# Query transposes and output stores first in a chunk, loads held until a chunk begins, scores three half heads to a gap, in a fused attention and feed-forward kernel

## Chip, cores and metric

One core of a Trainium2 chip. The metric is the device time of one execution in us. Times of one kernel are compared with times of the kernel before taken in the same rounds on the same chip. Besides that, the granted TensorE clock of each run (1.0 is full speed) is used.

## The reference, cut to what matters

```python
# q, k, v: (8 batches, 8 heads, 576, 64); 4608 tokens of width 512; hidden width 1536
k_p = k.reshape(B, H, 72, 8, D).mean(axis=3)        # keys and values pooled by 8
v_p = v.reshape(B, H, 72, 8, D).mean(axis=3)
attn = softmax(q @ k_p^T / sqrt(D))                 # 576 x 72 per head
x = (attn @ v_p), heads side by side                # 4608 x 512
out = (relu(x @ w_gate) * (x @ w_val)) @ w_out      # 4608 x 512
```

## The kernel before

The feed-forward part runs in nine chunks of 512 tokens. While PE (TensorE) works through the units of chunk c, the attention of batch c + 1 is slipped into the gaps between units, and GpSimd (POOL) pools the keys and values of batch c + 2. A unit is one group of feed-forward matmuls, either for a block of the hidden layer or for a part of the output. From batch 2 on queries are transposed by DMA from SyncE's queue, and from batch 3 on so is each finished piece of attention on its way to `x_T`; before that TensorE transposes most of them. Names in the profile lines: qT are transposed queries, kp and kpT pooled keys, expT exponentials of the scores, px a finished piece of attention, h the hidden layer.

```python
ps_mm = tile_pool(bufs=4, PSUM); ps_at = tile_pool(bufs=3, PSUM)   # ps_at: scores and values

def scores(b, h):                       # one head = two halves, one PSUM tile each
    e = exp_pool.tile([P, 2, HS], F16, name="expT")
    for j, parts in enumerate(...):
        ps = ps_at.tile([P, 512], F32, ...)
        ...matmuls...
        nc.scalar.activation(out=e[:SP, j, :], in_=ps[:SP, :HS], func=AF.Exp, ...)

def values(b, t):                       # one piece of 128 (or 64) tokens: two PSUM tiles
    for half in range(2):
        ps = ps_at.tile([P, 512], F32, ...)
        ...four matmuls...
        nc.vector.reciprocal(...); nc.vector.tensor_tensor(out=x[...], in0=pv, in1=rd, op=mult)

def attention(b):                       # what goes into which gap
    ...
    if b == 2:
        pairs = [Sc[h:h + 2] for h in range(0, H, 2)]       # two heads to a gap
        ...
        return [[], [kt], []] + pairs + [v[:1], v[1:2], x[:1] + v[2:], x[1:2], x[2:], V[3:4], V[4:]]
    return [[kt], []] + [[p] for p in Sc + V]
...
for c in range(1, n_chunks):
    ...
    if c + 2 < B: prep(c + 2, c + 3 < B)                    # POOL: pooling, loads
    if c + 1 < B: others = attention(c + 1)
    if c + 2 < B: others[-1].append(lambda: q_dma(c + 2))   # query transpose, last gap
    for i, unit in enumerate(units):
        unit()
        ...run(sums[2 * i - 2:2 * i])                       # VectorE: eight sums of h
        if i < len(others): run(others[i])
```

The softmax here doesn't subtract the row's maximum and nothing guards it: scores larger than these inputs give would overflow.

## Time and profile before

| | before |
|---|---|
| device time, first three runs | 339.09, 339.21, 341.12 us |
| the profiled run | 341.79 us, span 340.0 us, clock 0.995 |
| PE busy | 96% of the span |
| work of a chunk with attention that waits for nothing | 33.80 us |
| excess of chunks 2, 3, 4 over it | 4.52, 0.76, 0.50 us |

The prediction shows the lines that the argument rests on. Part 2 of the page gives the wider view; each digit is the busy share, or the granted clock, of one of 40 slices of the span:

```profile
PE   7899999999969999999999999999999999999994
...
POOL 8446509999999900992199830000000000000000
PEclk9999999999979999999999999999999999999999
```

Between the start and the tail PE's row and the clock row have one dip each, both in slice 12; they are the hole in chunk 2 and what follows it. POOL runs as far ahead as its buffers let it and is finished by slice 24.

### The profile page before, as it was taken

To read this page: it belongs to the slowest core of one execution; us is meant where nothing else is said; L and a number is where in the kernel's file an instruction comes from. 1 tells how busy PE (TensorE), PEld (TensorE's weight loads), DVE (VectorE), ACT (ScalarE), POOL (GpSimd) and SP (SyncE) were. 2 spreads that over 40 slices of the span, in tenths; PEclk is the share of its full clock that TensorE was granted. 3 is DMA by queue.
4 is the path that set the end of the run, shared out by engine and by line. 5 is a ranking of instruction groups with operands and counts; after the bars stand their busy time and mean duration, and the time that the engine had idled before them with its cause. 6 is when DMAs were issued, how large, how long until landed. Compare 5 with 4: busy or idle time off the path is not lost.

```text
span 340.0 us, 6437 instructions
## 1 busy us (share of the span) xinstructions
PE 326.3 (96%) x2502; PEld 211.1 (62%) x2502; DVE 212.8 (63%) x450; ACT 128.4 (38%) x276; POOL 137.2 (40%) x182
## 2 busy tenths in 40 slices
PE   7899999999969999999999999999999999999994
PEld 2588875544536665666898866665666565555542
DVE  7465636759757676867675775677567554486520
ACT  1544562464236324632463246324632322232221
POOL 8446509999999900992199830000000000000000
PEclk9999999999979999999999999999999999999999
DMA  7999999946968099837990380037003600400143
GB/s 109 191 203 201 195 212 171 184 96 124 139 117 163 10 143 132 147 60 125 168 164 12 79 155 24 17 75 173 4 9 57 129 1 0 124 3 2 36 114 97
DMA packets 50550, 35.41 MB, mean 104 GB/s; under 512 B 30360, under 2 KB 44184, under 8 KB 50520
## 3 DMA queue, kind: packets, MB, share of 16 engines
q0 software_dynamic: 18304, 18.88, 34.8%
q1 hardware_dynamic: 32072, 16.00, 23.5%
q8 instruction: 19, 0.31, 0.4%
q10 hardware_dynamic: 144, 0.13, 0.1%
q14 instruction: 11, 0.09, 0.1%
HBM read 37.75 MB, written 9.44 MB: 139 GB/s over the span
## 4 chain that ended last, share of the span: by engine, by line
PE 87%; DMA 6%; DVE 2%; ACT 1%; issue 1%; POOL 1%; DVEq 0%; ACTq 0%; POOLq 0%
PE mm_ps L415 51%; PE acc_ps L515 18%; PE mm_ps L462 5%; DMA qT<-q 5%; PE at_ps L304 4%; PE at_ps L374 3%; DMA q<-in_q_dram 2%; DVE px L380 1%; PE mm_ps L564 1%; PE mm_ps L397 1%; PE mm_ps L278 1%; ACT expT L308 1%; DVE h L433 1%; PE mm_ps L327 1%; PE mm_ps L351 1%
## 5 line engine op out<-in xcount | busy, mean ns | idle before, releaser
L433 DVE TENSOR_TENSOR h<-mm_ps,relu 128x512 f16<-128x512 f32 (+2 forms) x120 | 76.7, 640 | 80.3 <-PE mm_ps L415 77.3
L421 ACT ACTIVATE relu<-mm_ps 128x512 f16<-128x512 f32 (+1 forms) x120 | 66.5, 554 | 129.6 <-PE mm_ps L415 128.9
L415 PE MATMUL mm_ps<-x_T,wv_sb 128*128 128x512 f16 (+1 forms) x528 | 113.7, 342 | 0.5 <-DVE h L433 0.5
L415 PE MATMUL mm_ps<-x_T,wg_sb 128*128 128x512 f16 (+1 forms) x528 | 114.0, 342 | 0.0
L415 PEld LDWEIGHTS <-wv_sb 128*128 128x128 f16 x528 | 51.7, 98 | 43.3 <-issue 1.9
L415 PEld LDWEIGHTS <-wg_sb 128*128 128x128 f16 x528 | 49.8, 98 | 28.2 <-issue 0.8
L308 ACT ACTIVATE expT<-at_ps 72x288 f16<-72x288 f32 x112 | 38.9, 403 | 26.3 <-PE at_ps L304 26.3
L515 PEld LDWEIGHTS <-sum 128*128 128x128 f16 x336 | 32.6, 98 | 6.2
L380 DVE TENSOR_TENSOR px<-at_ps,prd 128x256 f16<-128x256 f32 (+1 forms) x80 | 33.8, 423 | 2.7
L178 POOL TENSOR_TENSOR tree_b<-tree_a 72x256 f32<-72x256 f32 (+1 forms) x42 | 32.1, 763 | 3.3
L515 PE MATMUL acc_ps<-wo_sums,sum 128*128 128x256 f16 x252 | 30.9, 273 | 0.0
L172 POOL TENSOR_TENSOR tree_a<-v_in 72x512 f32<-72x512 f16 x24 | 29.2, 1217 | 0.1
L515 PEld LDWEIGHTS <-h 128*128 128x128 f16 x252 | 24.0, 98 | 4.0
L172 POOL TENSOR_TENSOR tree_a<-k_in 96x512 f32<-96x512 f16 x18 | 21.0, 1168 | 12.1 <-DMA k_in<-in_k_dram 12.1
L515 PE MATMUL acc_ps<-wo_sb,h 128*128 128x256 f16 x168 | 20.6, 273 | 0.0
L462 PE MATMUL mm_ps<-wo_sb,h 128*128 128x512 f16 x84 | 19.6, 379 | 0.0
L506 DVE TENSOR_TENSOR sum<-h 128x768 f16<-128x768 f16 x28 | 17.7, 674 | 0.2
L164 POOL DMA_DIRECT2D q<-in_q_dram x9 | 5.1, 561 | 30.4 <-issue 16.3
L523 DVE TENSOR_TENSOR rows<-acc_ps,mid 128x512 f32<-128x512 f32 x21 | 14.4, 688 | 4.5 <-PE acc_ps L515 3.8
L374 PEld LDWEIGHTS <-expT 72*128 72x128 f16 (+1 forms) x280 | 13.0, 100 | 6.2 <-ACT relu L421 1.1
L379 DVE RECIPROCAL prd<-at_ps 128x4 f32<-128x4 f32 (+1 forms) x80 | 13.7, 171 | 3.7 <-PE at_ps L374 3.6
L374 PE MATMUL at_ps<-stat,expT 72*128 72x65 f16 (+1 forms) x280 | 14.8, 194 | 0.0
(92 smaller groups left out, 286.3 us busy)
## 6 DMA issues: line engine op xcount, KB each, us to landing
out_dram<-rows SPq DMA_DIRECT2D x24, 256.0 KB
k_in<-in_k_dram POOLq DMA_DIRECT2D x7, 576.0 KB, 6.5
q<-in_q_dram POOLq DMA_DIRECT2D x7, 576.0 KB, 9.4
v_in<-in_v_dram POOLq DMA_DIRECT2D x6, 576.0 KB, 13.0
out_dram<-fout SPq DMA_DIRECT2D x7, 256.0 KB
wg_sb<-in_moe_w_gate_dram POOLq DMA_DIRECT2D x6, 256.0 KB, 12.1
wv_sb<-in_moe_w_val_dram POOLq DMA_DIRECT2D x6, 256.0 KB, 12.1
wo_sb<-in_moe_w_out_dram POOLq DMA_DIRECT2D x3, 512.0 KB, 10.1
```

Source lines behind the costliest of these rows:

```text
L172: eng.tensor_tensor(out=cell["a"][:n], in0=src[:, :, :4 * D], in1=src[:, :, 4 * D:], op=ALU.add)
L178: eng.tensor_tensor(out=cell["c"][:n], in0=a[:n, :, :2 * D], in1=a[:n, :, 2 * D:], op=ALU.add)
L308: nc.scalar.activation(out=e[:SP, j, :], in_=ps[:SP, :HS], func=AF.Exp, scale=EXP_SCALE)
L374: nc.tensor.matmul(out=ps[:n, c0:c0 + D + 1], lhsT=weights(b, h, t), rhs=stats[b % 2][:SP, g, s0:s0 + D + 1], start=True, stop=True,)
L380: nc.vector.tensor_tensor(out=x[:n, half * NG // 2:(half + 1) * NG // 2, :, :], in0=pv.rearrange("p g (x c) -> p g x c", x=2)[:, :, :, :D] ...
L415: nc.tensor.matmul(out=t[:, lo:hi], lhsT=w[:, ci, fsl], rhs=x_T[:, ci, x0:x0 + hi - lo], start=(ci == 0), stop=(ci == n_co - 1),)
L421: nc.scalar.activation(out=relu[:, :n], in_=ps[0][:, :n], func=AF.Relu)
L433: nc.vector.tensor_tensor(out=h, in0=val, in1=relu, op=ALU.mult)
L462: nc.tensor.matmul(out=t, lhsT=h_tiles[c][:, fo, ts * P:(ts + 1) * P], rhs=wo_sb[:, fo, :], start=(fo == 0), stop=(fo == n_fo - 1),)
L506: nc.vector.tensor_tensor(out=S[k][:, i], in0=x[:, i], in1=y[:, i], op=op)
L515: nc.tensor.matmul(out=ps[:, tb, :], lhsT=lhs[:, i, tb * P:(tb + 1) * P], rhs=rhs[:, i, :], start=(first and tb == 0 and i == 0), stop=(tb ...
L523: nc.vector.tensor_tensor(out=out_ap, in0=x, in1=y, op=ALU.add)
```

## The change

The query transpose of batch c + 2 is moved from the last gap of chunk c to its second gap (batch 3's to the eighth gap of chunk 1), so that it is a whole chunk ahead. Loads are held behind a small copy on POOL until a chunk has begun, and output stores wait for the start of the next chunk, by intent to keep the transfers apart in time. Scores are cut into half heads and go three to a gap, which brings values forward; batch 2's last two values no longer fit into chunk 1 and go into chunk 2. The last chunk's rows get other buffers. The pooling of a batch (`prep`) is also issued later, before the fourth unit of a chunk and not before the first. The core, cut:

```diff
-    def scores(b, h):
+    def scores(b, h, j):                  # one half head
...
+                if last:
+                    o = half_pool.tile([P, 2, DM], F32, name=f"rows{ts % 2}", ...)[:, 0, :]
+                else:
+                    o = fout_pool.tile([P, DM], F32, name="fout")
...
+            if c + 2 < n_chunks:
+                sends.append(stores)
+            else:
+                stores()
...
+    def prep(b, load_next, behind=None):
...
+        if behind is not None:
+            nc.gpsimd.tensor_copy(out=gate, in_=behind)
         if load_next:
             load_k(b + 1)
...
-            pairs = [Sc[h:h + 2] for h in range(0, H, 2)]
+            trios = [Sc[i:i + 3] for i in range(0, 12, 3)] + [Sc[12:14], Sc[14:]]
...
-            return [[], [kt], []] + pairs + [
-                v[:1], v[1:2], x[:1] + v[2:], x[1:2], x[2:], V[3:4], V[4:]]
-        return [[kt], []] + [[p] for p in Sc + V]
+            return [[], [kt], []] + trios + [v[:1], v[1:2], x[:1] + v[2:], x[1:2], x[2:]], V[3:]
+        trios = [Sc[i:i + 3] for i in range(0, 2 * H, 3)]
+        return [[kt], []] + trios + [[p] for p in V], []
...
+                others, later = attention(c + 1)
+                for i, piece in enumerate(left):
+                    others[1 + i].insert(0, piece)
+                left = later
             if c + 2 < B:
-                others[-1].append(lambda: q_dma(c + 2))
+                others[7 if c == 1 else 1].append(lambda: q_dma(c + 2))
...
+                if i == prep_at and c + 2 < B:
+                    prep(c + 2, c + 3 < B, h_tiles[c][:, 1, :1] if c > 1 else None)
```

More of the change, by code (lines that the diff above doesn't have):

```diff
@@ L295 @@
     n_pc = 2 * NF + 1
-    def scores(b, h):
+    def scores(b, h, j):
         n = RI * QP
-        e = exp_pool.tile([P, 2, HS], F16, name="expT")
-        for j, parts in enumerate((((0, 0, NI),), ((0, NF * IQ, RI), (n, 0, NF * IQ)))):
-            ps = ps_at.tile([P, 512], F32, name="at_ps", tag="at_ps")
-            for c0, i0, cnt in parts:
-                nc.tensor.matmul(
-                    out=ps[:SP, c0:c0 + cnt * QP], lhsT=kpTs[b % 2][j][:, h, :],
-                    rhs=queries(b, h, i0, cnt), start=True, stop=True,
-                )
-            nc.scalar.activation(
-                out=e[:SP, j, :], in_=ps[:SP, :HS], func=AF.Exp, scale=EXP_SCALE)
-        exp_tiles[b, h] = e.rearrange("s j p -> s (j p)")
+        if j == 0:
+            exp_tiles[b, h] = exp_pool.tile([P, 2, HS], F16, name="expT").rearrange(
+                "s j p -> s (j p)")
+        parts = ((n, 0, NF * IQ), (0, NF * IQ, RI)) if j else ((0, 0, NI),)
+        ps = ps_at.tile([P, 512], F32, name="at_ps", tag="at_ps")
+        for c0, i0, cnt in parts:
+            nc.tensor.matmul(
+                out=ps[:SP, c0:c0 + cnt * QP], lhsT=kpTs[b % 2][j][:, h, :],
+                rhs=queries(b, h, i0, cnt), start=True, stop=True,
+            )
+        nc.scalar.activation(
+            out=exp_tiles[b, h][:SP, j * HS:(j + 1) * HS], in_=ps[:SP, :HS], func=AF.Exp,
+            scale=EXP_SCALE)
     def weights(b, h, t):
@@ L455, in out_rows @@
         cell = []
+        last = c == n_chunks - 1
         def part(lo, hi):
@@ L466, in part @@
             if hi == n_fo:
-                o = fout_pool.tile([P, DM], F32, name="fout")
+                if last:
+                    o = half_pool.tile(
+                        [P, 2, DM], F32, name=f"rows{ts % 2}", bufs=2 - ts % 2)[:, 0, :]
+                else:
+                    o = fout_pool.tile([P, DM], F32, name="fout")
                 if eng is nc.vector:
@@ L474, in out_rows @@
         return [lambda: part(0, n_fo // 2), lambda: part(n_fo // 2, n_fo)]
+    sends = []
     n_hf = n_fo // 2
@@ L525, in send, with stores @@
         def send(half):
-            for tb in range(2):
-                store(rows[half][:, tb, :], c * TCH + half * HT + tb * P)
+            def stores():
+                for tb in range(2):
+                    store(rows[half][:, tb, :], c * TCH + half * HT + tb * P)
+            if c + 2 < n_chunks:
+                sends.append(stores)
+            else:
+                stores()
         def pr1():
@@ L591, in load_wo @@
         )
-    def prep(b, load_next):
+    gate = const_pool.tile([P, 1], F16, name="gate")
+    def prep(b, load_next, behind=None):
         for i in range(KJ // 2):
             run(pool_k(b, i, nc.gpsimd))
+        if behind is not None:
+            nc.gpsimd.tensor_copy(out=gate, in_=behind)
         if load_next:
@@ L604, in scores_of @@
     def scores_of(b):
-        return [lambda h=h: scores(b, h) for h in range(H)]
+        return [lambda h=h, j=j: scores(b, h, j) for h in range(H) for j in range(2)]
     def values_of(b):
@@ L740 @@
         x = [lambda t=t: back(1, t, nc.scalar) for t in range(n_pc)]
-        run([z[3], z[4], z[5], a[6], qt[0], a[7], qt[1], qt[2], kt, z[6], z[7], a[8], Sc[0], Sc[1],
-             z[8], Sc[2], a[9], Sc[3], z[9], Sc[4], a[10], Sc[5], a[11], Sc[6], pv[0], z[10], Sc[7],
-             pv[1], z[11], V[4], o[0], V[0], x[4], o[1], V[1], x[0]])
+        run([z[3], z[4], z[5], a[6], qt[0], a[7], qt[1], qt[2], kt, z[6], z[7], a[8], *Sc[:4],
+             z[8], *Sc[4:6], a[9], *Sc[6:8], z[9], *Sc[8:10], a[10], *Sc[10:12], a[11], *Sc[12:14],
+             pv[0], z[10], *Sc[14:], pv[1], z[11], V[4], o[0], V[0], x[4], o[1], V[1], x[0]])
         q_dma(2)
@@ L747 @@
         prep(2, True)
+        left = []
         for c in range(1, n_chunks):
@@ L762 @@
             others = []
-            if c + 2 < B:
-                prep(c + 2, c + 3 < B)
-            if c + 1 < B:
-                others = attention(c + 1)
-            if c + 2 < B:
-                others[-1].append(lambda: q_dma(c + 2))
+            prep_at = 3
+            if c + 1 < B:
+                others, later = attention(c + 1)
+                for i, piece in enumerate(left):
+                    others[1 + i].insert(0, piece)
+                left = later
+            if c + 2 < B:
+                others[7 if c == 1 else 1].append(lambda: q_dma(c + 2))
             if c == 1:
@@ L776 @@
                     run(sums[2 * i - 2:2 * i])
+                if i in (0, 1) and sends:
+                    sends.pop(0)()
                 if i < len(others):
```

## The prediction

> **What bounds the kernel now.** I read the page first, for the engine that is full; then the PE timeline around each start of a chunk, because the change is about what is ready when a chunk starts; then PE's waits; then the DVE timeline beside the longest one. Part 1 of the page:
>
> ```profile
> PE 326.3 (96%) x2502; PEld 211.1 (62%) x2502; DVE 212.8 (63%) x450; ACT 128.4 (38%) x276; POOL 137.2 (40%) x182
> ```
>
> PE is busy 96% of 340.0 us, so the change can only win PE's holes and any slow clock: 13.7 us in all, of which 3.9 lie in the first 58 us and 5.1 in the tail after 324.55 (windows by stage), which the change hardly touches. To find the rest I take the seven key transposes (96x96, x7) that each chunk issues once, after its first unit, as a mark; the lines with a bracket are the score matmuls that PE waited for.
>
> ```profile
> 91.55 0.46 PE L248 MATMUL mm_ps<-ident,kp 96*128 96x96 f16 x7
> ...
> 97.73 0.42 PE L304 MATMUL at_ps<-qT,kpT1l 128*72 128x288 f16 x1 [2.68 <-DMA qT<-q]
> ...
> 129.87 0.46 PE L248 MATMUL mm_ps<-ident,kp 96*128 96x96 f16 x7
> ...
> 133.95 0.28 PE L304 MATMUL at_ps<-qT,kpT0l 128*72 128x288 f16 x1 [0.58 <-DMA qT<-q]
> ...
> 164.43 0.46 PE L248 MATMUL mm_ps<-ident,kp 96*128 96x96 f16 x7
> ...
> 198.73 0.46 PE L248 MATMUL mm_ps<-ident,kp 96*128 96x96 f16 x7
> ...
> 232.53 0.46 PE L248 MATMUL mm_ps<-ident,kp 96*128 96x96 f16 x7
> ```
>
> The reader sees periods of 38.32, 34.56, 34.30 and 33.80 us. The last, chunk 5, has no PE hole: 33.80 is what a chunk with attention costs. So chunks 2, 3 and 4 exceed it by 4.52, 0.76 and 0.50. Of chunk 4's 0.50, about 0.25 stays: its matmuls are cut in two at the ring's end, 1.75 instead of 1.73 us for a unit of eight, times 12. Chunk 2's 4.52 is more than its 2.68 of waiting; the clock shows why:
>
> ```profile
> 94.97:97.73 2.76, 0.08 (x2) 0.03 (x1) 2.73 (x4) 0.00 (x0) 2.65 (x3) 1.00 0.83 156
> 97.73:102.00 4.27, 4.27 (x18) 2.09 (x19) 0.72 (x2) 1.58 (x4) 4.13 (x6) 0.60 0.60 89
> ```
>
> (The column before the last two is the granted clock.) After the hole PE ran 4.27 us at 0.60: 4.27 x 0.40 = 1.7 us lost. Chunk 1's stretch has two more small holes:
>
> ```profile
> PE at_ps L304 <- ACT expT L308: 0.9, 4, 0.2
> ...
> PE mm_ps L415 <- DVE h L433: 0.5, 1, 0.5
> ```
>
> **What the Trainium skill says.** "TensorE: Matmul & The Clock Gate", What's actually happening: an idle window of some 3.4 us puts PE at half clock, and the windows run free. The trace agrees: 1.7 us lost at half clock is 3.4 us of it. "Perfetto Trace Analysis", Matmuls: independent groups should rotate through PSUM banks so that evacuation overlaps the next group. The before's score heads put four groups into three buffers, and the 0.9 above is that. "GPSIMD Engine Reference", Specifications: GpSimd shares SBUF interfaces with VectorE when a VectorE instruction has two SBUF inputs. The trace agrees: two of the 128x768 sums took 1.70 us with POOL busy (93.99) and 1.03 with POOL idle (132.31). "DMA: Bandwidth & Descriptors", Issuing engines are not separate DMA queues: all transfers share 16 engines. The trace agrees in that the query transpose lies between a busy POOL load stream and stores, but here the queue's order matters more than sharing.
>
> **The change, part by part.** I followed the instruction order and the waits of the changed program, with durations from the rows of the kernel before.
>
> 1. Query transposes first in a chunk. Batch 3's now goes out in the middle of chunk 1 rather than at 92.97, and every later one a whole chunk before its scores. The 2.68 and 0.58 waits for it go, with chunk 4's remaining 0.25 and the slow clock: up to 4.52 + 0.76 + 0.25 = 5.5 us.
>
> 2. Scores three half heads to a gap. Three groups for three PSUM buffers: in chunk 1 the four waits of 0.23 go, 0.9 us. The matmuls are the same. In later chunks one head's two halves already fitted, and ACT needs about 1.1 us for three exponentials (four took 1.30) against 1.3 to 1.7 of PE work in the next unit, so no gain and no loss.
>
> 3. Values sooner. With six gaps of scores instead of eight, values come two units earlier; their transposes had met the next chunk anyway (no PE wait for x_T in the trace), so nothing. In chunk 1 the new order spaces values and ACT copies such that the 0.48 wait on h should go: 0.5 us.
>
> 4. But batch 2 has no room for its last two values. They are put into chunk 2, in the gaps after its second and third units, the second of them ahead of the first three half heads. That costs a new wait, which I work out from PE's key transposes as zero. DVE from the before's rows:
>
> ```profile
> 91.82 0.69 DVE L433 TENSOR_TENSOR h<-mm_ps,relu 128x512 f16<-128x512 f32 x1 [1.03 <-PE mm_ps L415]
> 92.43 0.74 DVE L261 COPY kpT1l<-mm_ps 64x576 f16<-64x576 f16 x1
> 93.20 0.76 DVE L261 COPY kpT1u<-mm_ps 64x576 f16<-64x576 f16 x1
> 93.99 1.70 DVE L506 TENSOR_TENSOR sum<-h 128x768 f16<-128x768 f16 x2
> ```
>
>    So DVE has h at 0.9, both key copies at 2.4 and two sums at 4.1 (POOL is still pooling then, so the slow sums apply). Only then come the first moved values: 0.55 a half (86.95 to 88.05 for both halves in the before), done at 4.7 and 5.25. PE meanwhile: transposes 0.3, product 1.3, values 0.25, unit 1.73: at 3.6 it wants the other values. Their first half has the third buffer, the second must wait for 4.7, and the first score group for 5.25. The program gives the three score groups of this gap one and the same bank, since the other two hold values that DVE reaches only after h and two more sums; so each waits for the exponential before it: 0.78 us a step (a score at 65.48, its exponential from 65.80 for 0.41, and the wait's end). Scores go at 5.3, 6.1, 6.9, and the next unit starts at 7.0 instead of 3.6 + 0.25 + 0.36 = 4.2. New wait: 2.8 us, in pieces of at most 1.1. The two values themselves only move (0.5 us from chunk 1 to chunk 2).
>
> 5. Loads held. A one-column copy on POOL waits for h of a chunk's second unit, then the next batch's loads go. POOL's work for a batch is some 17 us (three trees of 2.45 for keys, four for values) in a chunk of 33.8, so pooled keys are ready about 10 us ahead. No gain on PE either way.
>
> 6. Stores first in a chunk, and the last chunk's rows in other buffers. No PE wait is put down to a store. In the tail ACT waited for one, here:
>
> ```profile
> 333.20 0.59 ACT L471 COPY fout<-mm_ps 128x512 f32<-128x512 f32 x1 [2.85 <-DMA out_dram<-fout]
> ```
>
>    Its matmuls ended near 332.3, so 0.8 us of it is real; its store then leaves earlier and crowds the two last ones less. The end hangs on the last half row (DVE at 334.98), so I give it 0.3 us.
>
> Sum: 0.9 + 0.5 (chunk 1) + 4.5 - 2.8 (chunk 2) + 0.76 + 0.25 + 0.3 = 4.4 us. 339.2 - 4.4 = 334.8.
>
> **Rivals.** (a) No new wait in chunk 2: the sum is 7.2 and the time 332.0, faster by 2.1%. For it: the change is evidently tuned for this spot, and were POOL idle at that moment the sums would end 0.7 sooner. Against: the buffer waits stand in the program, and even with fast sums 2.1 us of the 2.8 are left. (b) The new wait lets the clock drop as the old one did: PE is active for about 0.75 of 3.4 us there, against 0.6 in the old stretch, but spread. It costs 1.7 more: 336.5. I give it one chance in three; the windows run free, so it may differ between runs. (c) Held loads come too late, or collide with the transposes of x in mid chunk, and DVE waits for pieces: a wait of 1 us in five chunks would make 340. Against: the 10 us of slack above, and 1.7 MB at the 150 to 200 GB/s of the page takes some 10 us, over before most values are written. (d) The transfers were hidden anyway and only the wait's name changes: then chunk 2 alone decides and the time is about 337.
>
> **Range and chances.** Weighing 334.8 with a third of +1.7 and small tails from (a), (c) and (d): 335.1 us, a range of 332.2 to 338.0. Two per cent is 332.4, which needs (a) nearly whole: 0.12. Slower than 346 needs (c) several times over: 0.02. Within: 0.86.
>
> **What would show it.** The marks of the key transposes should be about 37 us apart from chunk 2 to chunk 3 (33.8 + 0.5 + 2.8), 33.8 from 3 to 4 and 34.05 from 4 to 5; PE's waits should name no qT transfer; at the start of chunk 2 PE's score and value matmuls should wait for DVE px and ACT expT, 2 to 3.5 us together; chunk 1's four waits of 0.2 should be gone; POOL's busy tenths should spread to about 240 us instead of ending near 200. I am wrong if chunk 2 comes out near 34.3 (no new wait: faster), if its clock falls to 0.6 again, or if later chunks lie above 34.1, which would be the held loads.

## The result, and the profile after

Six runs of the changed kernel: 335.05 to 337.34 us, median 336.32. Six of the kernel before: 339.09 to 342.93, median 341.13. The ratio is 0.9865, interval 0.9818 to 0.9912: a gain of 1.35%, within 2%. (A ratio is the mean time of one kernel's fast runs over that of the other's in the same rounds, so not quite the ratio of the medians.) Executions over 1.5% slower than the fastest of the same kernel are left out of the means. In later rounds (experiment 12) the same kernel gave 0.9892, interval 0.9858 to 0.9925.

The page of the changed kernel, parts 1 and 2:

```profile
PE 323.3 (97%) x2502; PEld 210.8 (63%) x2502; DVE 212.5 (64%) x450; ACT 127.4 (38%) x276; POOL 139.4 (42%) x186
...
PE   7899999999979999999999999999999999999994
...
POOL 8546509999999903990399039000000000000000
PEclk9999999999999999999999999999999999999999
```

PE's dip is still there, one tenth shallower; the clock's dip is not; POOL now works in bursts, one to a chunk, which is the held loads (the small copy at 129.59 us waited 12.43 us for h, and the loads follow it). The key transposes that serve as marks, in the PE timeline of the changed kernel:

```profile
88.44 0.46 PE L248 MATMUL mm_ps<-ident,kp 96*128 96x96 f16 x7
...
125.22 0.46 PE L248 MATMUL mm_ps<-ident,kp 96*128 96x96 f16 x7
...
159.02 0.46 PE L248 MATMUL mm_ps<-ident,kp 96*128 96x96 f16 x7
...
193.01 0.46 PE L248 MATMUL mm_ps<-ident,kp 96*128 96x96 f16 x7
...
226.78 0.46 PE L248 MATMUL mm_ps<-ident,kp 96*128 96x96 f16 x7
```

The periods are 36.78, 33.80, 33.99 and 33.77 us, against 38.32, 34.56, 34.30 and 33.80 before. Chunks 3 to 5 are free of holes. Chunk 2 is not: beyond 33.80 and the 0.5 us of values moved into it, 2.5 us are lost. The PE timeline at its start (the bracket is the idle time before the line and what ended it):

```profile
92.12 0.32 PE L377 MATMUL at_ps<-stat,expT 72*64 72x65 f16 x4
92.92 0.31 PE L377 MATMUL at_ps<-stat,expT 72*64 72x65 f16 x4 [0.48 <-DVE px L383]
93.47 0.31 PE L307 MATMUL at_ps<-qT,kpT1l 128*72 128x288 f16 x1 [0.23 <-DVE px L383]
94.28 0.29 PE L307 MATMUL at_ps<-qT,kpT1u 128*72 128x256 f16 x2 [0.49 <-ACT expT L311]
95.06 0.28 PE L307 MATMUL at_ps<-qT,kpT1l 128*72 128x288 f16 x1 [0.49 <-ACT expT L311]
```

No wait names qT any more. The values moved here wait for VectorE's px, and the three half heads go 0.8 us apart, each behind the exponential of the one before it, because all three were given one PSUM buffer: `ps_at` has three, and the other two held the second values, which VectorE read only from 95.33 and 95.87 us on, after the last of the three scores had started. What VectorE did meanwhile, in its timeline:

```profile
89.32 0.74 DVE L261 COPY kpT1l<-mm_ps 64x576 f16<-64x576 f16 x1
90.07 0.76 DVE L261 COPY kpT1u<-mm_ps 64x576 f16<-64x576 f16 x1
90.85 1.35 DVE L515 TENSOR_TENSOR sum<-h 128x768 f16<-128x768 f16 x2
...
92.99 0.42 DVE L383 TENSOR_TENSOR px<-at_ps,prd 128x256 f16<-128x256 f32 x1
93.33 0.68 DVE L436 TENSOR_TENSOR h<-mm_ps,relu 128x512 f16<-128x512 f32 x1
93.93 1.27 DVE L515 TENSOR_TENSOR sum<-sum,h 128x768 f16<-128x768 f16 x2
...
95.33 0.42 DVE L383 TENSOR_TENSOR px<-at_ps,prd 64x256 f16<-64x256 f32 x1
...
95.87 0.42 DVE L383 TENSOR_TENSOR px<-at_ps,prd 64x256 f16<-64x256 f32 x1
```

It is never idle: key copies, two sums, and only then the moved values. The last step to read is chunk 1. Between its key transposes and chunk 2's, one stretch of the windows view for each kernel; the columns are length, then busy time and count of PE, PEld, DVE, ACT and POOL, then clock, DMA share and GB/s. Before:

```profile
61.70:91.55 29.85, 28.45 (x190) 14.58 (x189) 22.24 (x47) 13.53 (x30) 28.11 (x37) 1.00 0.79 135
```

After:

```profile
61.70:88.44 26.74, 26.74 (x174) 14.13 (x173) 19.34 (x38) 13.72 (x30) 25.23 (x32) 1.00 0.93 167
```

(The changed kernel's own mark stands at 61.75, so its stretch is 26.69.) 3.11 us gone, with sixteen matmuls (0.5 us, the moved values) moved to chunk 2. The sum of the profiles: 3.1 in chunk 1, 1.5 in chunk 2, 0.8 and 0.3 in chunks 3 and 4, 0.9 from chunk 5 to the end, of which the tail has 0.8; together 6.6 of 340.0.

The two profiles differ by more than the mean times do, since the trace of before fell on one of its longer runs (341.79 us). Times of the changed kernel fall in two groups by the mean clock of the run: of twelve runs in two sets of rounds, eight at a clock of 0.998 or more took 335.05 to 335.88, and four at 0.993 or 0.994 took 336.56 to 337.34. The kernel before spreads from 337.9 to 342.9 over all rounds, with clocks from 0.991 to 1.0 where they are listed; only one of its runs has a trace, so which of its holes vary is not shown.

### The profile page after: what moved, and what is told of

The parts are those of the page before. It is cut to its first block, busy times and chain, and to the rows that moved or that the text cites.

```text
span 333.4 us, 6441 instructions
## 1 busy us (share of the span) xinstructions
PE 323.3 (97%) x2502; PEld 210.8 (63%) x2502; DVE 212.5 (64%) x450; ACT 127.4 (38%) x276; POOL 139.4 (42%) x186
## 4 chain that ended last, share of the span: by engine, by line
PE 93%; DVE 3%; DMA 2%; issue 1%; POOL 1%; ACT 0%; DVEq 0%; POOLq 0%
PE mm_ps L418 56%; PE acc_ps L524 19%; PE mm_ps L466 6%; PE at_ps L307 4%; PE at_ps L377 3%; DMA q<-in_q_dram 2%; DVE px L383 1%; PE mm_ps L580 1%; PE mm_ps L400 1%; PE mm_ps L354 1%; PE mm_ps L278 1%; PE mm_ps L330 1%; PE mm_ps L248 1%; PE mm_ps L242 0%; POOL k_in L144 0%
## 5 line engine op out<-in xcount | busy, mean ns | idle before, releaser
L418 PEld LDWEIGHTS <-wg_sb 128*128 128x128 f16 x528 | 48.5, 98 | 28.5 <-issue 0.8
L311 ACT ACTIVATE expT<-at_ps 72x288 f16<-72x288 f32 x112 | 38.1, 403 | 16.8 <-PE at_ps L307 16.8
L383 DVE TENSOR_TENSOR px<-at_ps,prd 128x256 f16<-128x256 f32 (+1 forms) x80 | 33.8, 423 | 2.7
L515 DVE TENSOR_TENSOR sum<-h 128x768 f16<-128x768 f16 x28 | 19.0, 720 | 0.1
L617 POOL COPY gate<-h 128x1 f16<-128x1 f16 x4 | 1.5, 381 | 39.2 <-DVE h L436 39.2
L377 PE MATMUL at_ps<-stat,expT 72*128 72x65 f16 (+1 forms) x280 | 14.8, 194 | 0.5 <-DVE px L383 0.5
```

Source lines behind the costliest of these rows:

```text
L311: nc.scalar.activation(out=exp_tiles[b, h][:SP, j * HS:(j + 1) * HS], in_=ps[:SP, :HS], func=AF.Exp, scale=EXP_SCALE)
L377: nc.tensor.matmul(out=ps[:n, c0:c0 + D + 1], lhsT=weights(b, h, t), rhs=stats[b % 2][:SP, g, s0:s0 + D + 1], start=True, stop=True,)
L383: nc.vector.tensor_tensor(out=x[:n, half * NG // 2:(half + 1) * NG // 2, :, :], in0=pv.rearrange("p g (x c) -> p g x c", x=2)[:, :, :, :D] ...
L418: nc.tensor.matmul(out=t[:, lo:hi], lhsT=w[:, ci, fsl], rhs=x_T[:, ci, x0:x0 + hi - lo], start=(ci == 0), stop=(ci == n_co - 1),)
L515: nc.vector.tensor_tensor(out=S[k][:, i], in0=x[:, i], in1=y[:, i], op=op)
```

## The experiments

Each is an edit of the changed kernel, or, where said, of the kernel before. All gave correct results. Experiments 1 to 4, 5 to 7 with 10, and 8, 9, 11 and 12 ran in three sets of rounds on three chips, so times are compared within a set or by their ratio to the kernel before. Medians are of fast runs. "Period of chunk 2" is the time from its key transposes to those of chunk 3, in each run's own trace.

**1. VectorE's sums behind the values of the gap, in chunk 2 alone.**

```diff
+                if c == 2 and i < len(others):
+                    run(others[i])          # before the sums, not after
                 ...run(sums[2 * i - 2:2 * i])
```

> Changed kernel, but in chunk 2 alone VectorE gets the values and the key copies of a gap before its two sums instead of after them. Theory (the new wait is made of two parts: VectorE's queue ahead of the moved values, and three half heads chained on one PSUM bank): the waits on px (0.48 and 0.23) go, the chain of exponentials stays. Marks of the key transposes from chunk 2 to chunk 3: 36.78 falls to about 35.6 (33.8 + 0.5 moved values + about 1.3 of chain). Time about 1.2 us under the changed kernel's. Rival (the wait is really for the query transfer or for late keys): period stays at 36.8.

Period of chunk 2: 35.81. The two waits on px are gone and the two on exponentials stay, as the PE timeline shows:

```profile
93.56 0.31 PE L307 MATMUL at_ps<-qT,kpT1l 128*72 128x288 f16 x1
94.37 0.28 PE L307 MATMUL at_ps<-qT,kpT1u 128*72 128x256 f16 x2 [0.49 <-ACT expT L311]
95.14 0.28 PE L307 MATMUL at_ps<-qT,kpT1l 128*72 128x288 f16 x1 [0.49 <-ACT expT L311]
```

Median 335.01, ratio 0.9875; the changed kernel did not run in these rounds, so the 1.2 us expected in time is not tested. The new wait has two parts, and VectorE's order is one.

**2. The second moved values in a gap of their own.**

```diff
                 others, later = attention(c + 1)
+                if c == 2:
+                    others.insert(2, [])
```

> Changed kernel, but in chunk 2 alone the second moved values have a gap of their own and all score groups come one gap later; VectorE's order stays. Theory: the wait of the second values' half on the first ones' px stays (0.5 to 0.65), and the scores, one unit later, still find one bank held by values that VectorE reaches after two sums, so one or two waits of 0.5 to 1 us remain: period from chunk 2 to 3 about 35.5 to 36. Rival (only the crowding of five groups in one gap matters): the period falls to 34.3, no waits.

Period of chunk 2: 35.81; one wait of 0.5 on px, one of 0.5 on an exponential, one of 0.3 on the key copies in chunk 1. The rival that only crowding matters falls. Median 335.56, ratio 0.9892.

**3. Both edits.**

> Both edits together. Theory: no PE wait at the start of chunk 2; period from chunk 2 to 3 is 33.8 + 0.5 = 34.3; 2.5 us under the changed kernel's undisturbed runs (335.4 by their mean), so about 332.9; and with no hole left, the granted clock is 0.999 to 1.000 in every run, so the runs at 0.994 (mean 337.1) vanish and the spread falls under 1 us. Rival for the clock (it drops for some reason of its own, not because of the hole): half of the runs still at 0.994.

This missed: period of chunk 2 35.86, not 34.3. Two waits on px were left, 0.78 and 0.23. The VectorE timeline of this run says why:

```profile
91.73 0.42 DVE L383 TENSOR_TENSOR px<-at_ps,prd 128x256 f16<-128x256 f32 x1
92.08 2.14 DVE L515 TENSOR_TENSOR sum<-h 128x768 f16<-128x768 f16 x2
94.14 0.68 DVE L436 TENSOR_TENSOR h<-mm_ps,relu 128x512 f16<-128x512 f32 x1
...
95.47 0.42 DVE L383 TENSOR_TENSOR px<-at_ps,prd 64x256 f16<-64x256 f32 x1
95.81 1.01 DVE L515 TENSOR_TENSOR sum<-sum,h 128x768 f16<-128x768 f16 x2
```

I had moved the first two sums behind the first values, but they still stood ahead of the second ones, and they took 2.14 us there while the next two took 1.01. Median 334.56, ratio 0.9862; no fast run below a clock of 0.997.

**4. Idle matmuls in the hole.** Three 128x512 matmuls on zeros ahead of each of the four pieces of the third gap.

```diff
+                    if c == 2 and i == 2:
+                        for piece in others[i]:
+                            warm(3)
+                            piece()
```

> Changed kernel with twelve 128x512 matmuls on zeros put into the wait of chunk 2 (three ahead of the second values and three ahead of each of the first three half heads). They compute nothing that is used. They take 12 x 0.216 = 2.6 us of PE, nearly all within the holes. Theory (the slow runs are the clock dropping after the hole): the clock is 1.000 in all runs, the period stays at 36.8 to 37.4, the time is 335.4 to 336.0 in all runs with no runs at 337. Rival (runs at 0.994 have another cause, or the matmuls just cost time): runs at 0.994 stay, or the period grows by 2.6 us.

The clock was 0.998 in the profiled run and 1.000 in the five others, and none fell to 0.994; but the period of chunk 2 was 37.55, a little above the 37.4 that I allowed, and the times were 335.79 to 337.36, median 336.54, where 335.4 to 336.0 were expected. So keeping PE busy went with an undisturbed clock, and nothing was won. By itself this run does not settle the clock: the matmuls also change the time, and six runs without a drop, where four of twelve had one, may be chance. Experiment 7 shows the drop directly.

**5. The kernel before with only the query transposes moved.**

```diff
-                others[-1].append(lambda: q_dma(c + 2))
+                others[8 if c == 1 else 1].append(lambda: q_dma(c + 2))
```

> Kernel before with one edit: the query transposes go out early (in chunk 1 at its ninth unit, later at the second unit of a chunk); loads not held, scores, values and stores as before. Theory (the wait for the query transfer was its place in the queue and in the program): no PE wait names qT; periods from chunk 2 on 33.8, 33.8 and 34.05; 5.5 us off the 340.0 of the profile, ratio near 0.985, as good as the whole change, because the change gives back 2.5 us in chunk 2. Rival (the transposes were slow because loads run beside them, so the loads must be held for it to work): PE waits on qT of 1 us or more stay, ratio 0.99 to 1.

The four fast runs took 335.61 to 336.84, ratio 0.9905. The profile fell on a slow run (344.74 us) and is used for chunk 2 alone, which ended before the disturbance; its marks in the PE timeline:

```profile
91.85 0.46 PE L248 MATMUL mm_ps<-ident,kp 96*128 96x96 f16 x7
...
125.65 0.46 PE L248 MATMUL mm_ps<-ident,kp 96*128 96x96 f16 x7
```

33.80: the whole excess of chunk 2 is gone with one moved call, with loads free and stores in their old places, and no PE wait names qT. The ratio of 0.985 that I expected is not reached; it was worked out from the one trace of before, which fell on a long run, and that is the likely reason, not a shown one. The intervals of this run (0.9861 to 0.9949) and of the whole change overlap. The changed kernel itself did not run in these rounds, but its near copies of experiments 6 and 7 did and gave 0.9880 and 0.9913: by these means most of the gain is this edit, and what the rest adds is not resolved.

**6. Loads not held.**

```diff
-                    prep(c + 2, c + 3 < B, h_tiles[c][:, 1, :1] if c > 1 else None)
+                    prep(c + 2, c + 3 < B, None)
```

> Changed kernel without the one-column copy on POOL that holds the loads. Theory: held loads win nothing on PE; periods as in the changed kernel (36.8, 33.8, 34.0, 33.8), time within 0.5 us of it (335.4 to 337). Rival: loads collide with transposes and stores, PE waits on qT or x_T appear, 1 to 3 us slower.

Six fast runs at 335.16 to 335.94 and one at 337.63 with a clock of 0.994: the changed kernel's two groups. The profile fell on a slow run again (347.89 us), whose disturbance lies in chunk 3. Chunk 2, before it, has the four waits of the changed kernel and a period of 38.42, with a slow clock (0.86 over 90 to 102 us) as in experiment 7; chunks 4 and 5 have 33.99 and 33.77, as there. Held loads won nothing that these times can show. (The later place of `prep` stayed, so only the copy is tested.)

**7. Stores as soon as the rows are there.**

```diff
-            if c + 2 < n_chunks:
-                sends.append(stores)
-            else:
-                stores()
+            stores()
```

> Changed kernel with the output stores issued as soon as their rows are there, as before. Theory: stores' place wins nothing on PE; periods and time as in the changed kernel within 0.5 us. Rival: stores in the middle of a chunk stand in the queue ahead of x transposes, and the next chunk's first matmul waits: periods above 34.1.

335.19 and 335.73 at a clock of 0.998, 336.96 to 337.59 at 0.994, four of six: again the two groups, in another mix, so the ratio of 0.9913 says little of the stores. Whether their place makes the slow clock rarer (four of six here, four of twelve in the changed kernel) is a rival that these few runs leave open. Its profile is of the second group and shows what I gave one chance in three. The stretch after the key transposes of chunk 2, at 88.57, in the windows view (clock third from the right):

```profile
88.00:92.00 4.00, 4.00 (x39) 2.62 (x37) 3.13 (x5) 1.59 (x3) 3.75 (x6) 1.00 0.38 96
92.00:100.00 8.00, 6.29 (x36) 3.38 (x35) 5.40 (x15) 2.89 (x8) 7.66 (x11) 0.79 0.62 102
100.00:127.03 27.03, 27.03 (x202) 16.60 (x200) 17.72 (x38) 9.76 (x22) 16.60 (x21) 1.00 0.55 111
```

The waits are those of the changed kernel to 0.1 us, yet the period is 38.46 instead of 36.78. The clock of 0.79 over 8 us is 1.7 us, which is the difference.

**8. Four half heads to a gap again in chunk 1.**

```diff
-            trios = [Sc[i:i + 3] for i in range(0, 12, 3)] + [Sc[12:14], Sc[14:]]
+            trios = [Sc[i:i + 4] for i in range(0, 16, 4)] + [[], []]
```

> Changed kernel, but chunk 1 has its score groups four to a gap again (two whole heads), with two gaps left empty so that all else stays in place. Theory (a wait costs more than its line says, because the line counts from the modelled end of the matmul before it, about 0.15 us after PE could take the next): the four waits of 0.23 come back, 0.9 by the lines, and chunk 1's stretch between the key transposes of chunk 1 and chunk 2 grows from 26.7 by 1.5 us to 28.2. Rival (lines tell the whole loss): it grows by 0.9 to 27.6. Time 1.5 or 0.9 us over the changed kernel's of the same rounds.

The four waits came back. One of them in the PE timeline:

```profile
65.81 0.29 PE L307 MATMUL at_ps<-qT,kpT0u 128*72 128x256 f16 x2
65.94 0.29 PE L307 MATMUL at_ps<-qT,kpT0l 128*72 128x288 f16 x1
66.46 0.28 PE L307 MATMUL at_ps<-qT,kpT0u 128*72 128x256 f16 x2 [0.23 <-ACT expT L311]
```

Half heads start 0.13 apart; the fourth starts 0.52 after the third. The loss is 0.39, the line says 0.23: it counts from the modelled end of the matmul before (65.94 + 0.29), but PE could have taken the next one 0.16 earlier. Times four that is 1.6 us, not 0.9. The stretch grew by more than I had expected, from 26.7 to 29.13, and the whole to a ratio of 1.0009, because the two gaps left empty moved other work too: values in chunk 1 had to wait, once 0.38 on px by the line and 0.54 from start to start, and chunk 2 had its waits and the slow clock (0.77 over 6 us). So the size of the four waits is shown, and the total of this run is not a price of the four alone.

**9. The last rows in the old buffers.**

```diff
-                if last:
+                if last and False:
```

> Changed kernel, but the last chunk's rows go into the two old row buffers again, so that the third waits for the first one's store. Theory (the tail's 0.8 us was won by the rows' own buffers): ScalarE's wait of 2.85 on a store comes back, and from the first matmul of the last rows to the end of the span it is 15.6 us as before instead of 14.8; time 0.3 to 0.8 over the changed kernel. Rival (the tail's 0.8 is chance in the last store's landing): 14.8 or scattered, with the wait there.

As expected. ScalarE's line in this run, and no such wait in the changed kernel:

```profile
328.22 0.58 ACT L479 COPY fout<-mm_ps 128x512 f32<-128x512 f32 x1 [2.85 <-DMA out_dram<-fout]
```

From the first matmul of the last rows (319.40) to the end of the span (335.0) it is 15.6 us, as in the kernel before; in the changed kernel 14.8 (318.61 to 333.4). PE's part is the same in both; the last store lands sooner. Beside the changed kernel in the same rounds (without each one's single run at 0.992 to 0.994) the means are 336.32 and 335.67.

**10. Moved values in gaps of their own, and the sums behind both.** What experiment 3 lacked.

```diff
+                if c == 2:
+                    others.insert(2, [])
...
+                if c == 2 and i < len(others):
+                    run(others[i])
                 if c == 1:
                     run(sums[i:i + 1])
-                elif i:
+                elif c == 2 and i > 1:
+                    run(sums[2 * i - 4:2 * i - 2])   # one unit later
+                elif c > 2 and i:
                     run(sums[2 * i - 2:2 * i])
```

> Changed kernel, in chunk 2 alone: the second moved values have a gap of their own, and VectorE's eight sums start one unit later, behind both moved values. The run with both earlier edits kept a loss of 1.2 to 1.5 us (waits of 0.78 and 0.23 on px) because two sums took 2.14 us between the two pairs of values. Theory (VectorE's queue is all that is left of the new wait): no PE wait above 0.2 at the start of chunk 2, period from chunk 2 to 3 is 34.3 to 34.6, clock 0.997 or more, time 2.3 us under the changed kernel's undisturbed 335.4, so about 333.1, ratio to before near 0.981. Rival (the sums come too late for the product that needs them): a new wait of up to 1 us at an acc_ps product, period 35 to 35.5.

The trace has no PE wait at all from 60 to 330 us. The three half heads at the start of chunk 2 go 0.13 apart:

```profile
94.53 0.29 PE L307 MATMUL at_ps<-qT,kpT1l 128*72 128x288 f16 x1
94.66 0.29 PE L307 MATMUL at_ps<-qT,kpT1u 128*72 128x256 f16 x2
94.80 0.29 PE L307 MATMUL at_ps<-qT,kpT1l 128*72 128x288 f16 x1
```

Period of chunk 2: 34.50, which is 2.28 less than in the changed kernel, as expected. Times 333.11, 333.19, 333.49, one of 336.87 at a clock of 0.997 and two slow ones; ratio 0.9838, interval 0.9784 to 0.9893, which the records call unclear. Three of four fast runs lie some 2.3 us under the changed kernel's first group (335.05 to 335.88), which ran in other rounds.

**11 and 12. The same version and the changed kernel once more, in the same rounds.**

> The version with the moved values in gaps of their own and the sums one unit later, again, beside the changed kernel on the same chip. Theory: no PE wait in chunk 2, 2.2 us under the changed kernel's undisturbed runs and more against its mean, since no hole lets the clock drop: 333.1 to 333.5 in undisturbed runs, ratio to before 0.980 to 0.984; no runs at a clock of 0.994 to 0.996 except those that one transfer holds up.

> The changed kernel again, for the same rounds. Theory: two groups of times, about 335.3 at a clock of 0.997 or more and about 337.1 at 0.993 to 0.995, the latter with 1.7 us of slow clock behind the hole of chunk 2; ratio to before 0.986 to 0.991.

The version: 334.06 to 334.89 in five fast runs and a slow one, ratio 0.9855 (0.9822 to 0.9888). The changed kernel: 335.41 to 335.87 in five runs and 336.56 at a clock of 0.994, ratio 0.9892 (0.9858 to 0.9925). The means are 334.57 and 335.82: still the faster of the two, every fast run of it below every run of the other, but by 1.25 us and not 2.2. The expected 333.1 to 333.5 was missed. The trace of the version has period 34.50 for chunk 2 without a wait, as before, and in chunk 3 a PE wait of 1.8 behind VectorE, which had waited 4.0 us for a DMA transpose of x to free its piece. The intervals of the two kernels overlap, so the order of the two rests on the runs of each group and on the traces.

**What stays open.** In slow runs (one each in experiments 2, 3, 6 and 11, two each in 5 and 10, at least one of before, none of twelve of the changed kernel) the two that have a trace show VectorE waiting some ten us for a transpose of x. In experiment 5:

```profile
161.39 0.42 DVE L380 TENSOR_TENSOR px<-at_ps,prd 64x256 f16<-64x256 f32 x1 [9.46 <-DMA x_T<-px]
```

Why the transpose is late there, and whether loads held or stores deferred make it rarer, these runs are too few to say.

## Why the prediction was right

The time, 336.32, lies in the range of 332.2 to 338.0, and the ratio, 0.9865, is close to the 0.988 of 335.1 over 339.2. By its steps:

1. *Query transposes.* Right: no qT wait, periods of 33.80 and 33.99 in chunks 3 and 4 where 33.8 and 34.05 were foretold. Experiment 5 shows it alone. That the chosen trace of before was a typical one was assumed and is not: runs of before come down to 337.9.
2. *Three half heads, and values sooner, in chunk 1.* Right in kind, too small: 1.4 us plus 0.5 moved stood in the sum, 3.1 were measured in the first trace (2.7 in the second, 62.02 to 89.18). The mis-sized term is four waits times 0.23: experiment 8 shows 0.39 each. That is 0.6 of the missing 1.2. The PE timelines of before, read from start to start, give most of the rest: the wait on h cost 0.66 and not 0.48, and the third and the last values took 0.43 and 0.38 where values without a wait take 0.25.
3. *The new wait in chunk 2.* Right: 2.5 us for the 2.8 foretold, waiting for px and for exponentials in the order described. The sums took 1.35 and 1.27 where 1.70 was taken from before. Experiments 1 to 3 and 10 show its parts: undo VectorE's order or the crowded gap, and about 1 us goes; undo both fully, and it is gone.
4. *The clock, one chance in three.* Right: by their mean clock four of twelve runs of the changed kernel have it, though neither of its traces; experiment 7 shows 1.7 us in its trace.
5. *Loads held, stores first.* Nothing won on PE, as experiments 6 and 7 agree within the two groups. A slip beside it: POOL was to be busy until about 240 us, but its last burst is in slice 25 of 40, at 208, since chunk 5 is the last one to pool, and not chunk 6.
6. *The tail.* 0.8 instead of 0.3: the step that only the last half row sets the end is wrong, for that row's store lands sooner when the row before it has been stored sooner (experiment 9).

With the 1.2 us of chunk 1 and the 0.5 of the tail, 335.1 would have been 333.4, below all that was measured. So two errors partly cancelled: these two terms were too small, and the gain was read from a trace of a long run (341.79 us) and taken off a median of three runs (339.2). That the time came so close to 335.1 was in part luck. How long chunk 2's hole is in the shorter runs of before is not shown.

## What to carry to other kernels

A transfer that something waits for at the start of a stage belongs at the start of the stage before, ahead of whatever else uses its queue; moving that one call won, by mean times, most of what the whole change won. When work is pushed into an already full moment, follow each engine's order there: the moved values were cheap on PE, but stood behind VectorE's sums and took the PSUM banks of the next scores. And take a wait on PE from start to start of the matmuls around it, since the idle time in a line leaves part of it out.

## What the Trainium skill lacked or had wrong

- "Perfetto Trace Analysis", Tensor Engine Instruction: the page says that a matmul's end is estimated, not what that does to waits. Here a wait listed as 0.23 us cost 0.39 from start to start, four times in a row (experiment 8).
- "TensorE: Matmul & The Clock Gate", What's actually happening: the page speaks of an idle window of some 3.4 us. In the kernel before, the clock fell after a hole of 2.68 us. In experiment 7 it fell, for 1.7 us of loss, after a stretch of 3.06 us (92.25 to 95.31) in which no single idle time was over 0.5 us by its line; the windows view has PE busy for 1.35 us of it, and counted from start to start (0.13 for a score group, half of 0.25 for four value matmuls) it is an estimated 0.64, a fifth. The same stretch in both traces of the changed kernel went without a fall. Elsewhere the page mentions frequent short idle times; how busy is busy enough is not on it.
- "GPSIMD Engine Reference", Specifications: the page names the contention of GpSimd with VectorE instructions of two SBUF inputs, without a size. In experiment 3 two 128x768 sums took 2.14 us beside POOL additions of 1.15 and 0.92, and the next two 1.01 while a POOL addition of usually 0.72 took 1.70: once VectorE paid about 1.1 us, once POOL about 1.0. Which side waits is treated on another page of the skill, so only the size is new.
- "DMA: Bandwidth & Descriptors": no page gives the spread of a DMA transpose in a shared queue; here one held up VectorE by 4.0 us in a fast run and by 9.5 and 10.3 us in two slow ones.
